# Attention and a gated feed-forward layer on one core: the mixture of v written in the queries' order by TensorE, w_spatial rounded on ScalarE, and new keys for the order of issue

## The chip, the cores and the metric

The kernel runs on one core of a Trainium2 chip. The metric is the device time of one execution in microseconds (us), as the median of several runs. A profile is one more execution, recorded by the hardware; its span runs from the first to the last recorded instruction. In the profile PE is TensorE, DVE is VectorE, ACT is ScalarE, POOL is GpSimd and SP is SyncE, which issues the DMAs.

## The reference

Eight batches of twelve heads attend over 448 positions with head size 64; the result, 448 x 768 for each batch, goes through a gated feed-forward layer. All inputs and outputs are float32.

```python
scores = matmul(q, k.T) / 8
scores = cap * tanh(scores / cap)
attn = exp(scores - max(scores)) / (sum + 1e-9)
x = matmul(attn, v)                      # heads side by side: (8, 448, 768)
h = maximum(x @ w_in, 0)                 # (8, 448, 1024)
u, v = h[..., :512], h[..., 512:]
v_n = (v - mean(v)) / sqrt(var(v) + 1e-6)
v_s = einsum('ts,bsd->btd', w_spatial, v_n) + b_spatial[None, :, None]
out = (u * v_s) @ w_out                  # (8, 448, 768)
```

## The kernel before

Two heads make a pair; there are 48 pairs, six to a batch. `pair_bnd` builds the work of a pair and `moe` that of a batch's feed-forward layer. Neither issues anything: each calls `add` with an engine, a duration, a key, what the task depends on and which buffers it takes. `Plan.order` then runs through a model of the engines and issues, on each engine, the ready task of least key, so that the keys, the durations and the buffer counts fix the order of instructions on every engine before the kernel runs. Keys come from the pair's number and a table (`BND_KEY`, with `KEY0` added in the first batch). TensorE works in two modes: attention matmuls on 64 x 64 tiles of the array (mode "K") and feed-forward matmuls on the whole array (mode "N"). The model adds `TURN` when the mode changes, and `STICK` to the key of a task that would change it.

The work of a pair, in blocks of 64 keys (seven blocks, `NC`), is this. The scores (line 548) go to the PSUM tile ps_s, of which there are two; ScalarE takes the tanh (line 555) and then, over half of the keys at a time, the exponential (line 560) into a tile tp. TensorE sums exp times v over the blocks into ps_x (line 570), of which there is one, and ScalarE copies it to xf (line 575). The order of the queries within qk2 is chosen on the host (`qp`, line 876), so that VectorE can find the maximum over keys by elementwise steps, a 32 x 32 transpose and a reduction (lines 590 to 600, tile red). The sum over keys is found in the same way, but in the first eight pairs (`PE_SUMS`) TensorE makes it with a matrix of ones (line 612, to ps_acc), and ScalarE copies it to sx (line 616, recorded at the helper's line 311). Maximum and sum cross the partitions by four small DMAs (md, dt, rd, rr), after which VectorE multiplies xf by rr (line 661), and xf is split into two rounded parts xg: a copy on ScalarE (line 662, recorded at line 311) and a difference on VectorE (line 663, recorded at line 307).

Since the queries come in another order than the output wants, the two copies out of PSUM put them back:

```python
out=xf.t.rearrange("p (i h b) -> p h b i", h=2, b=QB // 2), in_=x.t[:, :, :QH].rearrange("p h (b i) -> p h b i", i=32)
```

For the feed-forward layer of a batch TensorE makes u (lines 694 to 696), v (lines 716 to 721), the spatial product (lines 785 to 790) and the output (lines 810 to 812). Before the first of these the weights have to be split: w_in and w_out by `split_f64`, w_spatial by `split_f32`, whose four roundings to ws_h run on VectorE (line 338).

Of the kernel before, what the change touches and what calls it, by code (L numbers as in the profile page):

```python
# [42 lines left out]
class Plan:  # L43
# [7 lines left out]
    TURN, STICK = {"N": 200.0, "K": 150.0, "R": 190.0, "C": 145.0, "Q": 130.0}, 8.1  # L51
# [19 lines left out]
    def order(self):  # L71
# [35 lines left out]
        while done < len(self.tasks):  # L107
# [87 lines left out]
def gpc(n):  # L195
# [7 lines left out]
U_LEAD = 2  # L203
MOE_TAGS = {
    "xg": (XW, F32R, 8), "u": (448, F32, U_LEAD), "vh": (512, F32R, 4), "vl": (512, F32R, 4),
# [11 lines left out]
    "sx": (448, F32, 1), "v": (2 * NC * D, F32, 2), "tp": (2 * PW, F32, 4),  # L217
# [19 lines left out]
E_SEV = "A"  # L237


def attn_moe(ctx, tc, bounded, shared, qk, v, qk2, v2, cap, w_in, w_sp, w_out, out):  # L240
# [88 lines left out]
    def split_f32(key, c):  # L329
# [8 lines left out]
        b = add("V", dve2(S), key, lambda: nc.vector.tensor_copy(hi, t.t[:, :S]), [a], [t])  # L338
# [181 lines left out]
    def pair_bnd(b, hp, xf, rr):  # L520
# [3 lines left out]
        kk = lambda name, n=0: at + KEY[name] + KEY["step"] * n + (KEY0.get(name, 0.0) if b == 0 else 0.0)  # L524
# [7 lines left out]
        x, tps, exps, prev = Buf("x"), [], [], None  # L532

# [5 lines left out]
        for j in range(2):  # L539
            tp = Buf("tp")  # L540
# [62 lines left out]
        row = lambda y: y.rearrange("(e p c) -> p e c", e=2, c=QB)  # L603
# [289 lines left out]
```

## Time and profile before

| | us |
|---|---|
| median of 3 runs | 753.5 (752.08 to 755.51) |
| the profiled execution's own time | 750.37 |
| its span | 748.6 |
| TensorE busy in the span | 729.3 |
| VectorE busy | 616.5 |
| ScalarE busy | 495.7 |

The profiled execution lies 3.1 us under the median of the runs, and 1.8 us of its time lie around the span. A matmul in the profile begins before the one ahead of it has ended, so TensorE's busy time is not a sum of durations; the spacing from one start to the next is what a matmul costs in a row of them. Each attention matmul in the program is two matmul instructions in the profile, so a pair's 28 matmuls for scores, and its 28 for the mixture, are 56 there.

### The profile page before, as it was taken

How to read it: one execution, taken by the hardware profiler on the slowest of the kernel's cores; microseconds unless marked ns; L12 is line 12 of the kernel's file. 1: busy time of each engine (PE TensorE's matmuls, PEld its weight loads, DVE VectorE, ACT ScalarE, POOL GpSimd, SP SyncE). 2: the span in 40 equal slices, each digit the busy share in tenths (PEclk: the TensorE clock that was granted, in tenths of full speed). 3: DMA queues.
4: the chain of work that ended last, by engine and by line, in shares of the span. 5: the costliest groups of instructions: out<-in, count | busy, mean ns of one | idle time of the engine just before them, and what ended most of it. 6: DMA issues, size and time to landing. Idle time of an engine off the chain costs nothing.

```text
span 748.6 us, 18868 instructions
## 1 busy us (share of the span) xinstructions
PE 729.3 (97%) x7865; PEld 598.3 (80%) x7865; DVE 616.5 (82%) x1174; ACT 495.7 (66%) x658; POOL 62.4 (8%) x65
## 2 busy tenths in 40 slices
PE   7997999999999999999999999999999999999997
PEld 5865787886788878887788878888788877888896
DVE  4898899999999899867998599985999779986520
ACT  7999838669757584569855696557855698554321
POOL 3341211100100010000000001000010000100100
PEclk9999999999999999999999999999999999999999
DMA  7675613354222432234321352223322343112002
GB/s 247 183 219 170 230 47 126 95 166 138 76 66 86 144 103 76 65 113 138 114 63 36 135 160 77 66 87 128 115 65 72 125 133 115 42 28 89 13 2 79
DMA packets 51140, 79.22 MB, mean 106 GB/s; under 512 B 22882, under 2 KB 35684, under 8 KB 51044
## 3 DMA queue, kind: packets, MB, share of 16 engines
q1 hardware_dynamic: 51044, 77.91, 33.3%
q8 instruction: 64, 1.05, 0.6%
q14 instruction: 32, 0.26, 0.1%
HBM read 66.04 MB, written 11.81 MB: 104 GB/s over the span
## 4 chain that ended last, share of the span: by engine, by line
PE 67%; DVE 15%; DMA 11%; ACT 2%; issue 2%; POOL 1%; SPq 1%; DVEq 0%; ACTq 0%
PE ps_s L548 11%; PE ps_x L570 11%; DVE red L590 5%; PE ps_acc L810 4%; PE ps_acc L812 4%; PE ps_acc L811 4%; PE ps_acc L694 4%; PE ps_acc L695 4%; PE ps_acc L696 4%; PE ps_acc L719 3%; PE ps_acc L721 3%; PE ps_acc L720 3%; DMA rd<-dt 3%; DMA rr<-rd 3%; PE ps_acc L788 2%
## 5 line engine op out<-in xcount | busy, mean ns | idle before, releaser
L555 ACT ACTIVATE tp<-ps_s,capt 128x896 f32<-128x896 f32 x192 | 168.0, 911 | 20.6 <-PE ps_s L548 15.6
L548 PE MATMUL ps_s<-raw 64*64 64x224 f32 x2688 | 150.8, 355 | 8.3 <-ACT tp L555 8.1
L590 DVE TENSOR_TENSOR red<-red,tp 128x448 f32<-128x448 f32 (+1 forms) x176 | 148.0, 853 | 10.1 <-ACT tp L560 9.2
L560 ACT ACTIVATE tp<-tp,capt 128x1792 f32<-128x1792 f32 x96 | 154.2, 1606 | 2.2
L570 PE MATMUL ps_x<-tp,v 64*64 64x224 f32 x2688 | 145.5, 355 | 3.9 <-ACT xf L575 3.9
L548 PEld LDWEIGHTS ps_s<-raw 64*64 64x64 f32 x2688 | 98.1, 133 | 46.7 <-ACT tp L555 16.2
L570 PEld LDWEIGHTS ps_x<-tp,v 64*64 64x64 f32 x2688 | 103.6, 135 | 32.7 <-ACT xf L575 6.0
L590 DVE TENSOR_TENSOR red<-tp 128x896 f32<-128x896 f32 x88 | 93.1, 1076 | 22.6 <-ACT tp L560 22.6
L743 POOL TENSOR_TENSOR lst<-lst,capt 128x1 f32<-128x1 f32 x32 | 27.4, 857 | 561.3 <-DVE lst L741 547.1
L810 PE MATMUL ps_acc<-xg,wo_h 128*128 128x448 f32 x176 | 64.6, 367 | 0.1
L812 PE MATMUL ps_acc<-xg,wo_l 128*128 128x448 f32 x176 | 63.9, 363 | 0.0
L811 PE MATMUL ps_acc<-xg,wo_h 128*128 128x448 f32 x176 | 63.6, 361 | 0.0
L694 PE MATMUL ps_acc<-xg,wi_h 128*128 128x448 f32 x174 | 63.4, 364 | 0.0
L695 PE MATMUL ps_acc<-xg,wi_h 128*128 128x448 f32 x174 | 63.1, 363 | 0.0
L696 PE MATMUL ps_acc<-xg,wi_l 128*128 128x448 f32 x174 | 63.0, 362 | 0.0
L311 ACT COPY o<-ps_acc 128x448 f32<-128x448 f32 x44 | 23.4, 533 | 50.2 <-PE ps_acc L812 45.1
L598 DVE STREAM_TRANSPOSE red<-red 128x448 f32<-128x448 f32 x88 | 55.6, 634 | 0.8
L719 PE MATMUL ps_acc<-wi_h,xg 128*128 128x512 f32 x132 | 54.7, 414 | 0.0
L590 DVE TENSOR_TENSOR red<-red 128x448 f32<-128x448 f32 x88 | 53.7, 618 | 0.5
L575 ACT COPY xf<-ps_x 128x448 f32<-128x448 f32 x48 | 45.7, 951 | 12.0 <-DVE xg L307 5.1
L600 DVE TENSOR_REDUCE st<-red 128x14 f32<-128x448 f32 x88 | 51.5, 610 | 1.0
L720 PE MATMUL ps_acc<-wi_l,xg 128*128 128x512 f32 x132 | 52.2, 395 | 0.0
(116 smaller groups left out, 1147.7 us busy)
## 6 DMA issues: line engine op xcount, KB each, us to landing
raw<-in_qk SPq DMA_DIRECT2D x48, 448.0 KB, 3.9
v<-in_v SPq DMA_DIRECT2D x48, 448.0 KB, 4.1
rr<-rd SPq DMA_DIRECT2D x96, 112.0 KB, 2.8
out<-o SPq DMA_DIRECT2D x48, 224.0 KB, 2.0
w<-in_w_in SPq DMA_DIRECT2D x12, 512.0 KB, 4.7
xg<-in_w_out SPq DMA_DIRECT2D x12, 256.0 KB, 3.4
rd<-dt SPq DMA_DIRECT2D x48, 3.5 KB, 1.5
wy<-in_w_sp SPq DMA_DIRECT2D x3, 224.0 KB, 3.6
```

The source lines that it names most:

```text
L548: nc.tensor.matmul(ps.t[half_rows(h), e, c % 2 * QH:(c % 2 + 1) * QH], lhsT=raw.t[half_rows(e), S + c * D:S + (c + 1) * D], rhs=raw.t[half ...
L555: lambda o=g % 2 * PW, w=w, ps=ps, tp=tp: nc.scalar.activation(out=tp.t[:, o:o + 2 * w].rearrange("p (e q) -> p e q", e=2), in_=ps.t[:, :, ...
L560: lambda tp=tp, w=w: nc.scalar.activation(out=tp.t[:, :w], in_=tp.t[:, :w], func=AF.Exp, scale=ca), [ex], [tp],
L570: nc.tensor.matmul(x.t[half_rows(e), h, :QH], lhsT=vt.t[half_rows(h), (2 * c + e) * D:(2 * c + e + 1) * D], rhs=part(c, e)[half_rows(h)], ...
L590: tt = lambda o_, i0, i1, op=op: nc.vector.tensor_tensor(o_, i0, i1, op=op)
L694: nc.tensor.matmul(ps, lhsT=wi_h[:, c, fs], rhs=x[:, XH:], start=(c == 0), stop=False)
L695: nc.tensor.matmul(ps, lhsT=wi_h[:, c, fs], rhs=x[:, :S], start=False, stop=False)
L696: nc.tensor.matmul(ps, lhsT=wi_l[:, c, fs], rhs=x[:, XH:], start=False, stop=(c == NP - 1))
L719: nc.tensor.matmul(ps, lhsT=x[:, XH:][:, ts], rhs=wi_h[:, c, FH:], start=(c == 0), stop=False)
L810: nc.tensor.matmul(ps, lhsT=wo_h[:, c, ns], rhs=g[:, XH:], start=(c == 0), stop=False)
L811: nc.tensor.matmul(ps, lhsT=wo_h[:, c, ns], rhs=g[:, :S], start=False, stop=False)
L812: nc.tensor.matmul(ps, lhsT=wo_l[:, c, ns], rhs=g[:, XH:], start=False, stop=(c == 3))
```

## The change

Four things are changed. First, the matmuls of the mixture and of the sums write their output in the queries' own order: the host orders the queries so that each half of 224 stays together (`qp`), and the PSUM address steps by 7 elements, 28 bytes, from one column to the next (`inat`), where it stepped by one element before. The copies to xf and sx then read and write in order (sx in runs of seven elements), and the small DMA to rd moves runs of seven elements where it moved fourteen. Second, ScalarE rounds w_spatial. Third, the tile tp is split into tp for the first half of the keys and tq for the second, two buffers each in place of four, and u gets a third buffer. Fourth, the model of the engines and the keys have new numbers, and the second and the last batch have tables of their own beside the first.

```diff
-    TURN, STICK = {"N": 200.0, "K": 150.0, "R": 190.0, "C": 145.0, "Q": 130.0}, 8.1
+    TURN, STICK = {"N": 90.0, "K": 100.0, "R": 190.0, "C": 145.0, "Q": 130.0}, 12.24
...
-                    if e == "S":
+                    if e == "S" and took.dur:
                         dma = max(dma, took.end + 650.0) + took.lat + 300.0
-                        took.lat = dma + (1100.0 if took.lat > 1000.0 else 500.0) - took.end
+                        took.lat = dma + (1300.0 if took.lat > 1000.0 else 900.0) - took.end
...
-    "xg": (XW, F32R, 8), "u": (448, F32, U_LEAD), "vh": (512, F32R, 4), "vl": (512, F32R, 4),
+    "xg": (XW, F32R, 8), "u": (448, F32, 3), "vh": (512, F32R, 4), "vl": (512, F32R, 4),
...
-    "sx": (448, F32, 1), "v": (2 * NC * D, F32, 2), "tp": (2 * PW, F32, 4),
+    "sx": (448, F32, 1), "v": (2 * NC * D, F32, 2), "tp": (2 * PW, F32, 2), "tq": (PW + S, F32, 2),
...
+KEY1 = dict(ld=-4.24, vld=1.47, sc=-2.25, th=0.85, ex=-17.45, pv=-3.87, sm=-2.29, mx=-0.73, dn=-6.62, ev=-0.32, x=-5.3, moe=0.67, mv=-0.58)
+KEY7 = dict(ld=27.96, vld=8.74, sc=1.5, th=-0.21, ex=31.1, pv=18.57, sm=1.15, mx=0.16, dn=25.98, ev=42.09, x=22.77, moe=25.89, mv=8.24)
...
-        b = add("V", dve2(S), key, lambda: nc.vector.tensor_copy(hi, t.t[:, :S]), [a], [t])
+        b = add(E_WS, ct(E_WS, S), key, lambda: copy(E_WS, hi, t.t[:, :S]), [a], [t])
...
+        inat = lambda y: y.rearrange("p (i b) -> p b i", b=QB // 2)
+        hq = lambda y: y.rearrange("p (h q) -> p h q", h=2)
...
-                            nc.tensor.matmul(x.t[half_rows(e), h, :QH], lhsT=vt.t[half_rows(h), (2 * c + e) * D:(2 * c + e + 1) * D],
+                            nc.tensor.matmul(inat(x.t[half_rows(e), h, :QH]), lhsT=vt.t[half_rows(h), (2 * c + e) * D:(2 * c + e + 1) * D],
                                              rhs=part(c, e)[half_rows(h)], start=(c == 0), stop=(c == NC - 1))
...
-        z = add("A", act(S) + 420, kk("ev"), lambda: nc.scalar.copy(
-            out=xf.t.rearrange("p (i h b) -> p h b i", h=2, b=QB // 2), in_=x.t[:, :, :QH].rearrange("p h (b i) -> p h b i", i=32)), [prev],
-            [x, xf], [xf], name="xev")
+        z = add("A", act(S) + 45, kk("ev"), lambda: nc.scalar.copy(out=hq(xf.t), in_=x.t[:, :, :QH]), [prev], [x, xf], [xf], name="xev")
...
-                            nc.tensor.matmul(acc[h].t[half_rows(e), 0, :QH], lhsT=one[half_rows(h)], rhs=part(c, e)[half_rows(h)],
+                            nc.tensor.matmul(inat(acc[h].t[half_rows(e), 0, :QH]), lhsT=one[half_rows(h)], rhs=part(c, e)[half_rows(h)],
                                              start=(c == 0), stop=(c == NC - 1))
...
-            out=row(rd.t), in_=sec(0).rearrange("p (e c) -> p e c", c=QB)), [d], [dt], [rd], lat=XL)
+            out=row(rd.t), in_=sec(0).rearrange("p (e h b) -> p e h b", e=2, h=2)), [d], [dt], [rd], lat=XL)
...
-    qp = qt.reshape(B, H, D, 32, QB).transpose(0, 1, 2, 4, 3).reshape(B, H, D, S)
+    qp = qt.reshape(B, H, D, 2, 32, QB // 2).transpose(0, 1, 2, 3, 5, 4).reshape(B, H, D, S)
```

The numbers of matmuls, DMAs and vector instructions stay as they are, but for the four roundings that go from VectorE to ScalarE. The order changes everywhere. Three places follow; a count behind a row is of equal instructions in succession, 28 attention matmuls being one step of a pair.

On TensorE, in the middle of a later batch, the kernel before goes from the feed-forward matmuls (lines 785 to 790 and 694) to one pair's attention step and back. The rows are four attention rows between the last and the first feed-forward rows around them:

```order
L789 MATMUL ps_acc<-ws_l,vh 128x448
L790 MATMUL ps_acc<-ws_h,vl 128x448
L548 MATMUL ps_s<-raw_60 64x224 x16
L570 MATMUL ps_x<-tp,v 64x224 x16
L548 MATMUL ps_s<-raw_60 64x224 x12
L570 MATMUL ps_x<-tp,v 64x224 x12
L785 MATMUL ps_acc<-ws_l,vh 128x448
```

The changed kernel at the same point of a later batch (its lines are some five to seven further down: 555 for scores, 577 for the mixture, 791 to 796 for the spatial product):

```order
L796 MATMUL ps_acc<-ws_h,vl 128x448
L555 MATMUL ps_s<-raw_167 64x224 x12
L577 MATMUL ps_x<-tp,v 64x7x32 x16
L555 MATMUL ps_s<-raw_60 64x224 x16
L577 MATMUL ps_x<-tq,v 64x7x32 x12
L555 MATMUL ps_s<-raw_60 64x224 x12
L577 MATMUL ps_x<-tp,v 64x7x32 x16
L577 MATMUL ps_x<-tq,v 64x7x32 x12
L555 MATMUL ps_s<-raw_167 64x224 x16
L791 MATMUL ps_acc<-ws_l,vh 128x448
```

Where one visit held one pair's 56 matmuls, it now holds two pairs' 112, and the visits are fewer. Over the whole kernel TensorE goes from one mode to the other 83 times before and 61 times now.

On ScalarE, at the start, the kernel before has these rows after the two tanhs of the first half of pair 0 (tp is the scores' tile, sx the sums, xf the mixture):

```order
L560 ACTIVATE tp<-tp,capt 128x1792
L555 ACTIVATE tp<-ps_s,capt 128x896
L555 ACTIVATE tp<-ps_s,capt 128x448
L560 ACTIVATE tp<-tp,capt 128x1344
L555 ACTIVATE tp<-ps_s,capt 128x896 x2
L560 ACTIVATE tp<-tp,capt 128x1792
L311 COPY sx<-ps_acc 128x7x32 x2
```

And the changed kernel (562 is the tanh, 567 the exponential, 316 the copies):

```order
L567 ACTIVATE tp<-tp,capt 128x1792
L316 CAST ws_h<-wy 128x448
L562 ACTIVATE tq<-ps_s,capt 128x896
L316 CAST ws_h<-wy 128x448 x2
L562 ACTIVATE tq<-ps_s,capt 128x448
L562 ACTIVATE tp<-ps_s,capt 128x896
L567 ACTIVATE tq<-tq,capt 128x1344
```

Three of the four roundings of w_spatial now stand between the tanhs and exponentials of pair 0; the fourth comes after pair 2's.

On TensorE, in the last batch, the kernel before multiplies the sixth pair's part of x (xg_8290) into the first tile of v (ps_s_8258) after ten steps over the other five parts, which go to two tiles:

```order
L719 MATMUL ps_s_8279<-wi_h_156,xg_8213 128x512
L720 MATMUL ps_s_8279<-wi_l_157,xg_8213 128x512
L721 MATMUL ps_s_8279<-wi_h_156,xg_8213 128x512
L719 MATMUL ps_s_8258<-wi_h_156,xg_8290 128x512
L720 MATMUL ps_s_8258<-wi_l_157,xg_8290 128x512
L721 MATMUL ps_s_8258<-wi_h_156,xg_8290 128x512
```

The changed kernel does so (xg_8320 into ps_s_8245) only after all four tiles have had their five other parts:

```order
L721 MATMUL ps_acc_8314<-wi_h_159,xg_8274 128x512
L722 MATMUL ps_acc_8314<-wi_l_160,xg_8274 128x512
L724 MATMUL ps_s_8245<-wi_h_159,xg_8320 128x512
L725 MATMUL ps_s_8245<-wi_l_160,xg_8320 128x512
L726 MATMUL ps_s_8245<-wi_h_159,xg_8320 128x512
```

Ahead of these rows, since the last scores of the last pair, the kernel before has 72 output matmuls, 28 of the mixture and 30 of v; the changed one has 28 of the mixture, 48 of the output, 28 of the mixture and 55 of v.

## Rows read from the trace of the kernel before

**Rows 1.** Windows: stretch, its us, busy us by engine (instructions), granted clock, DMA share, GB/s.

```profile
4.90:90.14 85.24, 75.66 (x1448) 57.05 (x1448) 73.65 (x134) 79.04 (x103) 29.09 (x20) 0.94 0.71 222
60.00:80.00 20.00, 14.69 (x236) 10.18 (x232) 17.51 (x36) 17.31 (x25) 5.42 (x3) 0.83 0.61 197
90.14:743.00 652.86, 650.04 (x6412) 540.09 (x6408) 542.02 (x1035) 414.60 (x553) 33.12 (x41) 1.00 0.29 91
```

**Rows 2.** TensorE's waits to 90.14 us: who for whom, total us, times, longest.

```profile
PE ps_s L548 <- ACT tp L555: 6.1, 4, 3.3
PE ps_x L570 <- ACT xf L575: 3.4, 2, 2.0
```

**Rows 3.** TensorE's waits after 90.14 us.

```profile
PE ps_s L548 <- ACT tp L555: 1.9, 4, 1.1
PE ps_x L570 <- ACT xf L575: 0.4, 1, 0.4
```

**Rows 4.** Groups of ScalarE by shape: count, busy us, mean ns of one, idle before.

```profile
L555 ACT ACTIVATE tp<-ps_s,capt 128x896 f32<-128x896 f32 x144 | 141.2, 1003 | 20.5 <-PE ps_s L548 15.6 <-DVE red L590 3.5 <-PE ps_x L570 1.1
L560 ACT ACTIVATE tp<-tp,capt 128x1792 f32<-128x1792 f32 x48 | 86.0, 1792 | 1.1
L560 ACT ACTIVATE tp<-tp,capt 128x1344 f32<-128x1344 f32 x48 | 68.2, 1420 | 1.1
L575 ACT COPY xf<-ps_x 128x448 f32<-128x448 f32 x48 | 45.7, 951 | 12.0 <-DVE xg L307 5.1 <-DVE dt L634 3.7 <-PE ps_x L570 2.8
L311 ACT COPY o<-ps_acc 128x448 f32<-128x448 f32 x44 | 23.4, 533 | 50.2 <-PE ps_acc L812 45.1 <-ACT xg L311 2.6 <-DMA out<-o 2.5
```

**Rows 5.** Timeline of TensorE around two mode changes: start us, duration us, instruction.

```profile
343.53 0.39 PE L720 MATMUL ps_acc<-wi_l,xg 128*128 128x512 f32 x1
343.76 0.40 PE L721 MATMUL ps_acc<-wi_h,xg 128*128 128x512 f32 x1
344.09 1.74 PE L548 MATMUL ps_s<-raw 64*64 64x224 f32 x32
345.65 2.83 PE L570 MATMUL ps_x<-tp,v 64*64 64x224 f32 x56
348.30 1.31 PE L548 MATMUL ps_s<-raw 64*64 64x224 f32 x24
349.55 0.50 PE L719 MATMUL ps_acc<-wi_h,xg 128*128 128x512 f32 x1
```

**Rows 6.** Timeline of ScalarE at 42 us: start us, duration us, instruction.

```profile
40.47 1.79 ACT L560 ACTIVATE tp<-tp,capt 128x1792 f32<-128x1792 f32 x1
42.16 0.92 ACT L575 COPY xf<-ps_x 128x448 f32<-128x448 f32 x1
42.88 0.98 ACT L311 COPY sx<-ps_acc 128x224 f32<-128x224 f32 x2
43.66 0.63 ACT L311 CAST wi_h<-wy 128x512 fp32r<-128x512 f32 x1
...
45.95 0.57 ACT L311 CAST xg<-xf 128x448 fp32r<-128x448 f32 x1 [0.75 <-DVE xf L661]
46.42 0.63 ACT L555 ACTIVATE tp<-ps_s,capt 128x448 f32<-128x448 f32 x1
46.95 0.23 ACT L311 CAST xg<-xf 128x64 fp32r<-128x64 f32 x1
```

**Rows 7.** Timeline of TensorE where the last pair's scores end.

```profile
671.57 0.56 PE L548 MATMUL ps_s<-raw 64*64 64x224 f32 x8
...
672.37 0.37 PE L811 MATMUL ps_acc<-xg,wo_h 128*128 128x448 f32 x1
672.57 0.37 PE L812 MATMUL ps_acc<-xg,wo_l 128*128 128x448 f32 x1
```

**Rows 8.** Timeline where that pair's x is first used.

```profile
696.21 0.63 DVE L307 TENSOR_TENSOR xg<-xf,xg 128x448 fp32r<-128x448 f32 x1 [0.63 <-ACT xg L311]
...
697.05 0.39 PE L721 MATMUL ps_s<-wi_h,xg 128*128 128x512 f32 x1
```

More of the change, by code (lines that the diff above doesn't have):

```diff
@@ L224 @@
 ANY_W_KEYS = 2.0, 0.5, 8.0, 9.0, 1.0
-BND_KEY = dict(ld=-9.15, vld=0.69, sc=-2.3, th=36.27, ex=-132.38, pv=-0.12, sm=8.79, mx=10.7, dn=-1.77, ev=-20.83, x=-6.67, moe=11.19, span=6.93, step=0.15, mv=-18.73)
-KEY0 = dict(ld=-49.29, vld=2.7, sc=-103.24, th=-27.84, ex=31.5, pv=-29.52, sm=-1.19, mx=-50.91, dn=-18.09, ev=-50.06, x=-27.36, moe=-7.29, mv=5.22)
+BND_KEY = dict(ld=-71.91, vld=-26.44, sc=-4.99, th=45.96, ex=-129.9, pv=-0.09, sm=23.74, mx=23.02, dn=-17.91, ev=-77.3, x=-0.5, moe=11.36, span=8.83, step=1.3, mv=-12.86)
+KEY0 = dict(ld=-10.07, vld=2.24, sc=-114.04, th=-22.5, ex=63.83, pv=-24.18, sm=-41.18, mx=-48.52, dn=-59.88, ev=-2.76, x=-23.04, moe=-10.0, mv=5.36)
+KEY1 = dict(ld=-4.24, vld=1.47, sc=-2.25, th=0.85, ex=-17.45, pv=-3.87, sm=-2.29, mx=-0.73, dn=-6.62, ev=-0.32, x=-5.3, moe=0.67, mv=-0.58)
+KEY7 = dict(ld=27.96, vld=8.74, sc=1.5, th=-0.21, ex=31.1, pv=18.57, sm=1.15, mx=0.16, dn=25.98, ev=42.09, x=22.77, moe=25.89, mv=8.24)
 BND_V_FIRST = 1
 WARM, WARM_N = 9, 512
-BND_W_KEYS = -3.23, 2.34, -35.92, 5.87, -12.54
+BND_W_KEYS = -26.38, 3.1, -30.55, 8.66, -10.67
 PE_SUMS = 8
@@ L244, in attn_moe, with own @@
     PS = bass.MemoryType.PSUM
+    def own(b, name):
+        return {0: KEY0, 1: KEY1, B - 1: KEY7}.get(b, {}).get(name, 0.0) if bounded else 0.0
     def pool(name, bufs, space=None):
@@ L523, in pair_bnd @@
         at = b * H + 2 * hp
-        kk = lambda name, n=0: at + KEY[name] + KEY["step"] * n + (KEY0.get(name, 0.0) if b == 0 else 0.0)
+        kk = lambda name, n=0: at + KEY[name] + KEY["step"] * n + own(b, name)
         raw, vt = Buf("raw"), Buf("v")
@@ L539, in pair_bnd @@
         for j in range(2):
-            tp = Buf("tp")
+            tp = Buf("tq" if j else "tp")
             for g in (2 * j, 2 * j + 1):
@@ L602, in pair_bnd @@
                 [st] if a == 0 else [], name="red3"))
-        row = lambda y: y.rearrange("(e p c) -> p e c", e=2, c=QB)
+        row = lambda y: y.rearrange("(e h p b) -> p e h b", e=2, h=2, p=32)
         sums = None
@@ L611, in ones @@
                         for e in range(2):
-                            nc.tensor.matmul(acc[h].t[half_rows(e), 0, :QH], lhsT=one[half_rows(h)], rhs=part(c, e)[half_rows(h)],
+                            nc.tensor.matmul(inat(acc[h].t[half_rows(e), 0, :QH]), lhsT=one[half_rows(h)], rhs=part(c, e)[half_rows(h)],
                                              start=(c == 0), stop=(c == NC - 1))
             def sev(h):
-                copy(E_SEV, sx.t.rearrange("p (i h b) -> p h b i", h=2, b=QB // 2)[:, h],
-                     acc[h].t[:, 0, :QH].rearrange("p (b i) -> p b i", i=32))
+                copy(E_SEV, sx.t.rearrange("p (i h b) -> p h i b", h=2, b=QB // 2)[:, h],
+                     acc[h].t[:, 0, :QH].rearrange("p (i b) -> p i b", i=32))
             sums = add("T", NC * QQ, kk("pv", 1) + 0.01, ones, exps, [u, w, *acc], acc, name="ones", mode="K")
-            sums = [add(E_SEV, act(QH) + 210 if E_SEV == "A" else dve(QH), kk("ev"), lambda h=h: sev(h), [sums], [acc[h], sx], [sx] if h == 0 else [], name="sev")
+            sums = [add(E_SEV, act(QH) + 60 if E_SEV == "A" else dve(QH), kk("ev"), lambda h=h: sev(h), [sums], [acc[h], sx], [sx] if h == 0 else [], name="sev")
                     for h in range(2)]
@@ L659, in pair @@
         g = Buf("xg")
-        k += KEY["x"] + (KEY0["x"] if b == 0 else 0.0) if bounded else 1.3
+        k += KEY["x"] + own(b, "x") if bounded else 1.3
         m = add(E_X[0], st2(E_X[0], 448), k, lambda: eng[E_X[0]].tensor_tensor(xf.t, xf.t, rr.t, op=ALU.mult), deps, [xf, rr], name="xmul")
@@ L675, in moe @@
     def moe(b, xs):
-        k0 = (b + 1) * H + KEY["moe"] + (KEY0["moe"] if bounded and b == 0 else 0.0)
+        k0 = (b + 1) * H + KEY["moe"] + own(b, "moe")
         step = KEY["span"] / 18.0
@@ L682, in moe @@
         tags = iter(["s", "s", "acc", "acc"] * 5 if bounded and b == B - 1 else ["acc"] * 18)
-        kv = lambda k: k + KEY["mv"] + (KEY0["mv"] if bounded and b == 0 else 0.0)
+        kv = lambda k: k + KEY["mv"] + own(b, "mv")
         def u_part(js):
@@ L766, in v_part @@
                 vs.append((vh, vl, s4, s5 if last else None))
+        lead = U_LEAD0 if bounded and b < V_FIRST else U_LEAD
         if b >= V_FIRST:
             v_part()
-            u_part(range(U_LEAD))
+            u_part(range(lead))
         else:
-            u_part(range(U_LEAD))
+            u_part(range(lead))
             v_part()
         for j in range(4):
-            if j and j + U_LEAD <= 4:
-                u_part([j + U_LEAD - 1])
+            if j and j + lead <= 4:
+                u_part([j + lead - 1])
             k = next(ks)
```

4 lines of the change are left out of this document (2 added, 2 removed).

## Prediction

> **What bounds the kernel now.** I read the windows first, since the share of busy time hides two quite different stretches. From 90.14 us on, where the first feed-forward matmul starts, TensorE is busy 650.0 of 652.9 us at the full granted clock, and its waits there come to some 2.3 us, on ScalarE's tanh and on its copy to xf [rows 1, 3]. In that stretch only three things can change the time: how long a matmul takes, how often the mode changes, and a new wait.
>
> Up to 90.14 us it is otherwise. From 4.90 to 90.14 us ScalarE is busy 79.0 of 85.2 us, TensorE 75.7 and VectorE 73.7 [rows 1]. TensorE's waits there are 9.5 us, all on ScalarE: 6.1 us for a tanh that frees a scores tile, 3.4 us for the copy that frees the only ps_x [rows 2]. Its mean clock is 0.94, and 0.83 from 60 to 80 us, where part of the time it had the lower of its two levels, 1.2 GHz, after such waits [rows 1]. ScalarE sets the pace of this first stretch, TensorE that of the rest.
>
> Prices: four matmul instructions on 64 x 64 tiles run together, and 56 of them (14 such fours) take from 345.65 to 348.30, which is 0.189 us a four, 2.65 us for a pair's scores or mixture [rows 5]. Feed-forward matmuls are 0.20 us apart at 448 columns and 0.23 at 512 [rows 5, 7].
>
> **The change, part by part.** *Mode changes.* From the scores at 348.30 (six fours, 1.14 us) to the feed-forward matmul at 349.55 is 1.25 us, so 0.11 over; from the matmul at 343.76 to the scores at 344.09 is 0.33 in place of 0.23, so 0.10 over [rows 5]. A change costs 0.105 us, and 22 fewer save **2.3 us**. This is TensorE's own time in the stretch that it bounds.
>
> *Copies on ScalarE.* The copy to xf takes 951 ns on average, but what follows starts before its end: 42.16 to 42.88 is 0.72 us. A ScalarE operation on as many elements that reads and writes in order is a cast to xg, 0.47 us to the next start (45.95 to 46.42); the copy of an output tile takes 533 ns by its mean [rows 4, 6]. So each copy costs 0.25 us less by starts, 0.42 by durations. I take the starts. Two copies to sx cost 0.78 us (42.88 to 43.66) [rows 6]; half of 0.47 each, for half the columns, would be 0.47, and because their writes still step every seven elements I take 0.58, which saves 0.2 us a pair. Eight pairs lie in the first stretch: 8 x (0.25 + 0.2) = 3.6 us off ScalarE, against four roundings of 448 columns at 0.47 = 1.9 us put on it. Net **1.7 us** where ScalarE sets the pace. The lower end: if the three roundings between the tanhs of pair 0 hold up its scores while everything else is waiting for them, 1.4 us come back, and the net is 0.3. The upper end is 8 x (0.42 + 0.3) - 1.9 = 3.9 us. The four roundings leave VectorE, which does not set the pace; I count that as nothing, and it would be 1.9 us too if VectorE did.
>
> *After 90 us.* ScalarE is not the bound there (414.6 of 652.9 us busy), but the 2.3 us of waits are all on it, and each has one or two copies ahead of it that get shorter by 0.25. I take **1.3 us** of them back, between 0 and 2.3.
>
> *The strided write.* No row of this trace has TensorE write PSUM with a step, so I bound it by rates. An attention matmul writes 224 columns in the 0.189 us of a four, one element per partition and bank in 0.84 ns; a feed-forward matmul writes 448 in 0.20 us, one in 0.45 ns, or two adjacent elements in 0.90 [rows 5, 7]. If the cost is per pair of neighbouring elements, which the step makes into one each, the strided write needs one access in 0.84 ns where the densest row already makes one in 0.90. It fits, and I take **0**. The other end is a write at half the pace, 0.189 us more for each four. The mixture has 672 fours and the sums in eight pairs 112, so that end is 784 x 0.189 = 148 us. The Trainium skill ("PSUM — Partial Sum Buffer", Specifications (TRN2)) speaks against this change: it gives PSUM lines of 8 bytes and says that any non-contiguous access pattern slows matmuls significantly. By that sentence the kernel gets much slower; the rates of the rows leave room for the step, and no run here shows one yet. It is the first rival.
>
> *Visits of two pairs.* A pair's exponentials used to be ready a visit ahead; now the third block of scores of a visit waits for tanhs of the same visit. TensorE reaches it after 1.14 + 1.51 + 1.51 + 1.14 + 1.14 + 2.65 = 9.1 us. ScalarE begins some 1.0 us into the visit and has until then a tanh and a half (0.90 + 0.53), an exponential (1.32), two tanhs (1.80), a copy (0.47), an exponential (1.69) and a tanh (0.90): 7.6 us, so it is done at 8.6, and 8.8 with the handoff (durations less the 0.1 us by which the next start overlaps) [rows 4, 6]. It fits with 0.3 us left, and would not with the copy as it was. I take **0**; the bound is the second rival.
>
> *The last batch.* From the end of the last scores (671.57 + 0.38) to that pair's x is 24.9 us, as VectorE ends it at 696.84, and its first use is at 697.05: the kernel just gets by [rows 7, 8]. Now 28 + 28 attention matmuls, 48 of output and 55 of v stand in between: 5.3 + 9.7 + 12.8 + 0.3 = 28.1 us. So 3.2 us are to spare, which also covers the DMA to rd, whose pieces are half as long. Nothing is gained by it, because nothing waited. What is late next is the last tile of v, now finished with the first one; u follows on TensorE for 36 x 0.20 = 7.2 us, and I count this as even.
>
> *No cost elsewhere.* The split into tp and tq keeps four buffers, and the third buffer of u gives room only.
>
> Sum: 2.3 + 1.7 + 1.3 = 5.3 us off the profiled execution's 750.4 (span 748.6 and 1.8 around it) gives 745.1. The median of the runs lies 3.1 us above that execution, so **748.2 us**. A change of 0.5%, 3.8 us, is about what a measurement of this kernel can tell from none.
>
> **The rivals.** *The strided write is slow* (slower; place: the mixture and the sums). At half the pace: 748 + 148 = 896 us. It decides early: with 5.3 us of gain, 7 ns on each of the 784 fours (4%) bring the time back to that of before, and 12 ns (6%) make it slower by 0.5%. Against it speak the rates; for it, that no row of this trace holds a strided write, so nothing measured excludes it. The sentence of the Trainium skill ("PSUM — Partial Sum Buffer", Specifications (TRN2)) is on its side. Chance 0.13.
>
> *Visits of two pairs wait.* Eleven visits hold 112 attention matmuls. If a cast to xg and its small one (0.47 + 0.13) come between, the 0.3 us are gone and 0.3 us are lost; with VectorE late to free tp it may be 0.5: 11 x 0.5 = 5.5 us, about 753.7 us. It takes the place of the waits removed. Chance 0.13.
>
> *Only the mode changes count.* The roundings on ScalarE at the start, and a new order there with its own waits, eat the copies' gain: 751.2 us. For it speaks that TensorE waits for ScalarE from the first tanh on. Chance 0.17.
>
> *The first stretch is repaired.* ScalarE is idle 6.2 us of it, and TensorE loses up to 0.06 x 85.2 = 5.1 us to the lower clock [rows 1]. With an order that keeps both busy another 5 us go: 743 us. For it speaks that the mixture now comes before the sums, so that ps_x is freed earlier. Chance 0.20.
>
> **How the numbers follow.** The forecast has the rest, 0.37; its own range, from the bounds of the copies and of the waits, is 744 to 751. The range of 741 to 755.5 takes in the last three rivals but for their ends, and leaves out the slow write (0.13) and some 0.06 at the ends. Faster than 749.7: 0.29 of the forecast, 0.20 of the first stretch, 0.04 of the mode changes alone, 0.04 of the waiting visits (they may wait less), 0.57 together, and I say 0.58. Slower than 757.3: the slow write 0.13 and 0.03 of waiting visits, 0.16. The rest is 0.26.
>
> **What would show it.** The fours of the mixture and of the sums still 0.189 us apart, or not: that alone can make the prediction badly wrong. The copy to xf near 0.53 us on average. TensorE's waits up to the first feed-forward matmul under 9.5 us, and that matmul before 90 us by about two. In the middle, waits of TensorE for a tanh inside the visits would show the second rival, and none would show the working right; 0.105 us at each of 61 mode changes. In the last batch no wait before the last pair's x. The forecast would be wrong, too, if the lower clock came at other places: each microsecond at 1.2 GHz that TensorE has work in costs half of one.

## The result and the profile after

| | us |
|---|---|
| before, median of 5 runs | 753.5 (752.08 to 755.51) |
| after, median of 5 runs | 746.8 (743.99 to 749.32) |
| ratio after to before | 0.9912, 95% interval 0.9888 to 0.9936 |
| the profiled execution of after, its own time | 743.99 |
| its span | 742.0 |

The changed kernel is 0.9% faster: 746.8 us, 1.4 under the 748.2 forecast and inside its range, a gain of 6.7 us where 5.3 were forecast. The whole interval lies beyond the 0.5% that a measurement can tell. The profiled execution lies again below the median of the runs, by 2.8 us.

The same three windows, with the first feed-forward matmul now at 83.66 us (it was at 90.14), answer to [rows 1].

```profile
4.90:83.55 78.65, 70.63 (x1401) 52.75 (x1400) 63.44 (x119) 73.24 (x100) 17.14 (x18) 0.98 0.72 218
60.00:80.00 20.00, 17.23 (x356) 12.93 (x350) 17.05 (x34) 18.46 (x27) 3.84 (x3) 1.00 0.70 204
83.55:737.00 653.45, 649.26 (x6460) 543.91 (x6456) 543.91 (x1046) 406.01 (x562) 32.90 (x44) 1.00 0.31 94
```

The first stretch is 6.6 us shorter. It also holds less: 12 fours of attention (48 records, of which the window misses one: 1448 became 1401) now lie behind its end, 2.3 us of TensorE's work at 0.189 a four. The granted clock from 60 to 80 us is 1.00, where it was 0.83. The long stretch is no shorter.

TensorE's waits in the first stretch, and then those behind it, answer to [rows 2, 3].

```profile
PE ps_s L555 <- ACT tq L562: 7.0, 5, 2.6
PE ps_s L555 <- ACT tp L562: 0.4, 1, 0.4
...
PE ps_acc L699 <- ACT xg L316: 1.3, 1, 1.3
PE ps_acc L699 <- DVE stg L736: 1.0, 1, 1.0
PE ps_acc L796 <- DVE vl L312: 0.7, 1, 0.7
PE ps_acc L816 <- DVE o L801: 0.4, 1, 0.4
```

The wait for ps_x is gone, and no wait inside a visit of two pairs is in the list. The waits behind the first stretch are new ones. The sixteenth feed-forward matmul, the first that needs the last pair's xg, waits for it; later ones wait for stg, vl and o. Behind that xg stand a transfer, VectorE's product and ScalarE's cast, one after the other:

```profile
86.86 0.63 DVE L666 TENSOR_TENSOR xf<-xf,rr 128x448 f32<-128x448 f32 x1 [1.26 <-DMA rr<-rd]
...
87.58 0.71 ACT L316 CAST xg<-xf 128x448 fp32r<-128x448 f32 x2 [3.72 <-DVE xf L666]
...
88.20 0.47 PE L699 MATMUL ps_acc<-xg,wi_h 128*128 128x448 f32 x1 [1.26 <-ACT xg L316]
```

The groups of ScalarE by shape answer to [rows 4].

```profile
L562 ACT ACTIVATE tp<-ps_s,capt 128x896 f32<-128x896 f32 x96 | 91.9, 999 | 12.9 <-PE ps_s L555 6.8 <-PE ps_x L577 5.3 <-DVE red L595 0.6
...
L582 ACT COPY xf<-ps_x 128x448 f32<-128x448 f32 x48 | 25.5, 531 | 7.8 <-DVE xg L312 5.0 <-PE ps_x L577 2.5
L316 ACT COPY o<-ps_acc 128x448 f32<-128x448 f32 x44 | 23.3, 532 | 42.4 <-PE ps_acc L818 40.8 <-issue 1.1 <-ACT xg L316 0.5
...
L316 ACT COPY sx<-ps_acc 128x224 f32<-128x224 f32 x16 | 5.0, 368 | 0.8 <-PE ps_acc L617 0.7
```

The copy to xf takes 531 ns in place of 951, as the copy of an output tile does; the copy to sx takes 368 in place of the 574 of before:

```profile
L311 ACT COPY sx<-ps_acc 128x224 f32<-128x224 f32 x16 | 7.6, 574 | 0.6 <-PE ps_acc L612 0.6
```

The timeline of TensorE in a visit of two pairs shows the strided write.

```profile
343.73 1.69 PE L577 MATMUL ps_x<-tp,v 64*64 64x224 f32 x32
345.24 1.69 PE L555 MATMUL ps_s<-raw 64*64 64x224 f32 x32
346.75 0.56 PE L577 MATMUL ps_x<-tq,v 64*64 64x224 f32 x8
```

Eight fours of the mixture, written with the step, take 1.51 us, as do eight fours of scores, written without it: 0.189 us a four in both.

Where the 6.6 us of span went I read by adding up the distances from each start of a TensorE matmul to the next, from the first attention matmul to the last matmul of the program. The usual step of its kind is taken off each, and what is over is put down to a recorded wait, to a change of mode, or, in attention matmuls of over 450 ns, to the lower clock.

| us | before | after |
|---|---|---|
| usual steps | 703.8 | 704.1 |
| waits up to the first feed-forward matmul | 9.6 | 8.0 |
| waits behind it | 2.8 | 4.0 |
| lower clock | 7.1 | 3.1 |
| mode changes (83, then 61) | 8.5 | 6.4 |
| the rest | 5.9 | 5.6 |
| sum | 737.7 | 731.2 |

By this table mode changes gave 2.1 us, waits 0.4, and the lower clock 4.0, which the prediction did not have as a term. Each column is one execution. The experiments ask whether these are causes.

### The profile page after: what moved, and what is told of

Same layout as the page of the kernel before. It is cut to its first block, busy times and chain, and to the rows that moved or that the text cites. A ratio compares the mean times of both kernels' runs of the same rounds, so it can differ in the third digit from the quotient of the medians.

```text
span 742.0 us, 18882 instructions
## 1 busy us (share of the span) xinstructions
PE 723.6 (98%) x7865; PEld 597.9 (81%) x7865; DVE 608.1 (82%) x1170; ACT 481.2 (65%) x662; POOL 50.2 (7%) x65
## 4 chain that ended last, share of the span: by engine, by line
PE 82%; DVE 8%; DMA 6%; ACT 2%; issue 1%; SPq 1%; POOL 0%; DVEq 0%; ACTq 0%; POOLq 0%
PE ps_s L555 15%; PE ps_x L577 15%; PE ps_acc L816 5%; PE ps_acc L817 5%; PE ps_acc L818 5%; PE ps_acc L699 4%; PE ps_acc L724 4%; PE ps_acc L701 4%; PE ps_acc L700 4%; PE ps_acc L725 3%; PE ps_acc L726 3%; DMA rr<-rd 3%; DVE red L595 3%; PE ps_acc L794 2%; PE ps_acc L796 2%; PE ps_acc L795 2%
## 5 line engine op out<-in xcount | busy, mean ns | idle before, releaser
L595 DVE TENSOR_TENSOR red<-red,tq 128x896 f32<-128x896 f32 (+1 forms) x176 | 146.2, 846 | 43.1 <-ACT tq L567 42.9
L562 ACT ACTIVATE tp<-ps_s,capt 128x896 f32<-128x896 f32 x96 | 91.9, 999 | 12.9 <-PE ps_s L555 6.8
L567 ACT ACTIVATE tp<-tp,capt 128x1792 f32<-128x1792 f32 x48 | 86.5, 1802 | 0.6
L577 PE MATMUL ps_x<-tp,v 64*64 64x224 f32 x1536 | 81.8, 349 | 0.0
L562 ACT ACTIVATE tq<-ps_s,capt 128x896 f32<-128x896 f32 x96 | 74.7, 822 | 10.0 <-PE ps_s L555 9.2
L577 PEld LDWEIGHTS ps_x<-tp,v 64*64 64x64 f32 x1536 | 58.4, 133 | 14.9 <-issue 0.6
L567 ACT ACTIVATE tq<-tq,capt 128x1344 f32<-128x1344 f32 x48 | 68.1, 1419 | 1.3
L577 PE MATMUL ps_x<-tq,v 64*64 64x224 f32 x1152 | 63.5, 349 | 0.0
L748 POOL TENSOR_TENSOR lst<-lst,capt 128x1 f32<-128x1 f32 x32 | 24.4, 765 | 567.4 <-DVE lst L746 489.2
L316 ACT CAST xg<-xf 128x448 fp32r<-128x448 f32 (+1 forms) x96 | 35.0, 404 | 28.6 <-DVE xf L666 23.1
```

What stands on the lines that cost most here:

```text
L562: lambda o=g % 2 * PW, w=w, ps=ps, tp=tp: nc.scalar.activation(out=tp.t[:, o:o + 2 * w].rearrange("p (e q) -> p e q", e=2), in_=ps.t[:, :, ...
L567: lambda tp=tp, w=w: nc.scalar.activation(out=tp.t[:, :w], in_=tp.t[:, :w], func=AF.Exp, scale=ca), [ex], [tp],
L577: nc.tensor.matmul(inat(x.t[half_rows(e), h, :QH]), lhsT=vt.t[half_rows(h), (2 * c + e) * D:(2 * c + e + 1) * D], rhs=part(c, e)[half_rows ...
L595: tt = lambda o_, i0, i1, op=op: nc.vector.tensor_tensor(o_, i0, i1, op=op)
```

## The experiments

Medians are compared with runs of the kernel before on the same chip, given beside each. "First matmul" is the start of the first feed-forward matmul in the profile.

**The layout alone.** The new layout in the order of before, and with w_spatial still rounded on VectorE.

```diff
-                            nc.tensor.matmul(x.t[half_rows(e), h, :QH], lhsT=vt.t[half_rows(h), (2 * c + e) * D:(2 * c + e + 1) * D],
+                            nc.tensor.matmul(inat(x.t[half_rows(e), h, :QH]), lhsT=vt.t[half_rows(h), (2 * c + e) * D:(2 * c + e + 1) * D],
...
-            out=xf.t.rearrange("p (i h b) -> p h b i", h=2, b=QB // 2), in_=x.t[:, :, :QH].rearrange("p h (b i) -> p h b i", i=32)), [prev],
+            out=hq(xf.t), in_=x.t[:, :, :QH]), [prev],
...
```

> The layout alone (strided write by TensorE, copies in order, halves of the queries, small DMA) in the order of issue of the kernel before, word for word. Theory: the fours of mixture and sums stay 0.189 us apart, the copy to xf falls from 951 to about 530 ns, and ScalarE, which paces the first stretch, has about 3.6 us less there with no roundings added; the first feed-forward matmul comes 1.5 to 3.5 us before 90.1 and the time is 750 to 752 us (0.995 to 0.998 of before). Rival, that the whole gain is the order's: 753.5 us, ratio 1.000. Rival, that most of it is the layout's: under 749 us.

Measured: 754.45 against 754.17, ratio 1.0008 (0.9991 to 1.0024). The copies are short (523 and 362 ns), and nothing is gained. First matmul at 91.38 us, against 90.14. ScalarE's waits up to there show where the saving went.

```profile
ACT tp L557 <- PE ps_s L550: 5.1, 4, 4.4
ACT xg L311 <- DVE xf L663: 4.1, 3, 1.8
ACT tp L557 <- PE ps_x L572: 1.8, 1, 1.8
```

In before the wait for VectorE's xf was 1.1 us in all:

```profile
ACT xg L311 <- DVE xf L661: 1.1, 2, 0.7
```

ScalarE does 6.0 us less of copies up to that point (9.1 in place of 15.1), and its idle time grew by 4.9: from 6.2 by [rows 1] to 11.1, 75.4 busy of 86.5.

**The order alone.** The order of after, w_spatial on ScalarE, the layout of before.

```diff
-                            nc.tensor.matmul(inat(x.t[half_rows(e), h, :QH]), lhsT=vt.t[half_rows(h), (2 * c + e) * D:(2 * c + e + 1) * D],
+                            nc.tensor.matmul(x.t[half_rows(e), h, :QH], lhsT=vt.t[half_rows(h), (2 * c + e) * D:(2 * c + e + 1) * D],
...
-    qp = qt.reshape(B, H, D, 2, 32, QB // 2).transpose(0, 1, 2, 3, 5, 4).reshape(B, H, D, S)
+    qp = qt.reshape(B, H, D, 32, QB).transpose(0, 1, 2, 4, 3).reshape(B, H, D, S)
```

> The changed kernel's order of issue, with the layout of before (contiguous write by TensorE, copies out of PSUM that reorder). Theory: 61 mode changes as in the changed kernel, 2.1 us less than before; ScalarE has 3.6 us more in the first stretch than the changed kernel, and in the visits of two pairs TensorE waits 0.1 to 0.5 us for a tanh in several of the eleven, since the copy of 0.72 us does not fit; 749 to 752 us. Rival, that the order makes all of it: 746 to 747.5 us and no waits inside visits.

Measured: 749.98 against 754.17, ratio 0.9949 (0.9929 to 0.9969); first matmul at 86.88 us. So the layout alone is worth 0, the order alone 4 us, both 7: the short copies are worth about 3 us in the new order and nothing in the old. (What is called the order here holds the roundings on ScalarE, the split of tp and the third buffer of u as well; only the roundings are taken by themselves, below.)

In the profiles the first matmul lies 3.2 us behind after's. Of these, 1.7 are a slower stretch behind the wait for a tanh at 45 us: 64 attention matmul instructions take 4.77 us there, and 3.08 in after, with a granted clock from 40 to 60 us of 0.91 against 1.00. First after, then the order alone:

```profile
45.43 1.74 PE L555 MATMUL ps_s<-raw 64*64 64x224 f32 x32 [1.66 <-ACT tq L562]
...
45.66 2.90 PE L555 MATMUL ps_s<-raw 64*64 64x224 f32 x32 [2.22 <-ACT tq L562]
```

VectorE's waits up to 82 us differ between the two orders. First the kernel before, in which it waits for transfers and for GpSimd alone:

```profile
DVE ws_h L338 <- DMA wy<-in_w_sp: 5.5, 3, 4.6
DVE dt L634 <- DMA dt<-md: 3.2, 3, 1.8
DVE wy L380 <- POOL wy L376: 1.1, 2, 0.6
DVE xf L661 <- DMA rr<-rd: 0.9, 1, 0.9
```

Then the order alone, in which it waits for exponentials of ScalarE:

```profile
DVE red L595 <- ACT tp L567: 6.2, 1, 6.2
DVE red L595 <- ACT tq L567: 4.3, 2, 4.1
DVE dt L639 <- DMA dt<-md: 1.9, 3, 0.8
```

After has 6.0 and 4.0 in the two upper rows. In the order of before VectorE has no wait for ScalarE in this list, and with the short copies ScalarE waits 4.1 us for it. The 10 us of the new order are not the opposite of that: the two long waits end at 10.2 and 15.4 us, so they are for the first pair's exponentials, where before had the 5.5 us for w_spatial's transfer. Behind them VectorE waits at most 1.0 us at a time for ScalarE, and these lists do not show which engine sets the pace from there on.

**The roundings of w_spatial back on VectorE,** in after, at the same place of the order. It was run twice, the second time beside the changed kernel on one chip.

```diff
-    b = add(E_WS, ct(E_WS, S), key, lambda: copy(E_WS, hi, t.t[:, :S]), [a], [t])
+    b = add(E_WS, ct(E_WS, S), key, lambda: copy("V", hi, t.t[:, :S]), [a], [t])
```

> The changed kernel with the four roundings of w_spatial issued on VectorE at the same place of the order. Theory: TensorE's wait of 2.6 us at 8.6 us, which two of the roundings on ScalarE lengthen, falls to about 1.6; ScalarE has 1.9 us less to do in the first stretch; 745 to 746 us, 1 to 1.9 us under the changed kernel. Rival, that VectorE's queue is late in turn (maxima of pair 0, weights of w_in): the same time or up to 1 us more, the first feed-forward matmul not before 83.5 us.

> The changed kernel with the four roundings of w_spatial on VectorE at the same place of its order, for a profile nearer to its median than the one that the first such run left, and a comparison with the changed kernel on the same chip. Theory: the roundings cost ScalarE 1.9 us where it sets the pace and VectorE has room (5.8 of 15.1 us busy up to 20 us), so 1.5 to 3.5 us under the changed kernel (about 743.5), with the first feed-forward matmul 1 to 2 us earlier than the changed kernel's. Rival: the 3.5 us of the first comparison were a luckier clock; then the two are within 1 us.

Measured: first 743.33 against 754.17, ratio 0.9855 (0.9837 to 0.9872), then 745.26 against 752.96, ratio 0.9898 (0.9876 to 0.992). The profile of the first is of its slowest execution, and has the first matmul at 85.47 us, 1.5 to 1.8 behind the 83.66 and 83.97 of the changed kernel's two profiles. In that of the second it is at 81.83 us, 1.8 to 2.1 before them, and the window up to there shows ScalarE shorter by 2.3 and VectorE fuller by 2.7 than in after:

```profile
4.90:81.83 76.93, 69.88 (x1400) 53.97 (x1400) 66.12 (x124) 70.97 (x96) 16.79 (x18) 0.98 0.74 225
```

But on the one chip that both ran on, the time is the same (745.03 and 745.26). The 3.5 us of the first comparison did not come again. Two us in the first stretch are what one profile of two shows, so neither that the roundings cost them there nor that moving them shortens the whole is shown. In that one profile TensorE is still 1.7 us ahead of after's at 300 us, at the same matmul, and 0.5 behind at 492. That is no more than what two executions of one kernel differ by: the two profiles of the changed kernel itself drift 2.3 us apart behind the first matmul.

**The changed kernel again,** on that chip.

> The changed kernel itself on this chip, for a second profile and as the measure for the other runs of this call. Median 745 to 748. If the theory is right that its runs spread with how often TensorE falls to 1.2 GHz after a wait, the span is lower where the granted clock is higher, and the second profile shows such a stretch at other places than 12 us; the steps of mixture and sums stay at 0.189 us a four in every stretch at full clock.

Measured: 745.03 against 752.96, ratio 0.9886 (0.9862 to 0.991). First matmul at 83.97 us. The sums of the table above are here 8.6 and 4.9 us for waits up to and behind it, 3.7 for the lower clock, 6.4 for mode changes. So the new waits behind the first stretch, 4.0 and 4.9, belong to the kernel and not to one execution. (Of the 4.9, two are for a tanh, 0.7 and 0.3 us, both in visits shorter than two pairs.) That the span falls with the granted clock did not hold: its five spans of 741.8 to 744.5 had 0.997, 0.994, 0.993, 0.995 and 0.997, in this order.

**Long copies in the first batch only, and in the others only.** The order of after; `old(b)` picks the layout of before. The edit is that of the first run; in the other the condition is `n > 0`.

```diff
+old = lambda n: n == 0
...
-    inat = lambda y: y.rearrange("p (i b) -> p b i", b=QB // 2)
+    inat = lambda y: y.rearrange("p (i b) -> p b i", b=QB // 2) if not old(b) else y
...
```

> The changed kernel, order and all, but the six pairs of the first batch have the layout of before, so that their copies on ScalarE are long again (about 0.95 and 0.58 us); 42 pairs keep the short copies. Theory: the order alone was 3.2 us slower than order and layout together because the first stretch, up to the first feed-forward matmul, goes at ScalarE's pace. Six long copies to xf (0.25 us each by starts) and twelve to sx (0.1 each) are 2.7 us there, so the median should lie 2 to 3 us over the changed kernel (by 746.8: 749 to 750), and the first feed-forward matmul should come 2 to 3 us later than 83.7 us. Rival: the long copies hurt in the visits of two pairs, which are all later; then this run is within 1 us of the changed kernel on the same chip.

> The mirror image: the first batch has the short copies, the other 42 pairs the layout of before with the long ones. Theory (the first stretch goes at ScalarE's pace): 747 to 748, at most the 1.3 us that waits after the first stretch can give, and the first feed-forward matmul near 83.7 us. Rival (the visits of two pairs do not fit with long copies): 11 visits by 0.3 us and more, 3.3 us, about 750, with waits of TensorE for a tanh inside the visits.

Measured, against 745.03 of the changed kernel: 746.55 with the long copies first (to before 0.9923, 0.9894 to 0.9952), 747.95 with the long ones later (0.9939, 0.9912 to 0.9965). First matmul at 85.13 and 84.97 us, 1.0 to 1.5 us behind the changed kernel's two. The later copies that could count for this are those of the two pairs of the second batch that lie ahead of the first matmul. But the delay does not last. At the sixteenth feed-forward matmul, which waits for the last pair's xg in the changed kernel, the two are at 88.24 and 88.33 us, and the changed kernel's profiles at 88.20 and 88.25; the order alone, with all copies long, is at 90.73. And with the long copies first 1.7 us of delay are again a slower stretch behind the wait at 45.6 us (granted clock 0.91 from 40 to 60 us). The rival asked for waits inside the visits, and the waits of TensorE behind the first matmul, with the long copies later, have none of over 0.3 us for a tanh:

```profile
PE ps_acc L803 <- DVE vl L313: 0.6, 1, 0.6
PE ps_acc L707 <- DVE xg L313: 0.4, 1, 0.4
PE ps_s L556 <- ACT tp L563: 0.3, 1, 0.3
```

By this profile the visits fit with the long copies too. The place that the theory gave is not shown either: by the profiles neither half costs anything at 88 us. Of the medians, the 1.5 us with the long copies first are within the overlap of the two intervals, and the 2.9 us with the long ones later are just clear of it (0.9912 to 0.9965, against 0.9862 to 0.991). Where the short copies gain their 3 us stays open.

**The casts to xg of the first batch on VectorE,** so that ScalarE no longer stands at them; with the layout alone, and with nothing else changed in before.

```diff
+        E_C, E_C2 = ("V", "V") if bounded and b == 0 else (E_X[1], E_X[3])
...
-        c = add(E_X[1], ct(E_X[1], 448), k, lambda: copy(E_X[1], g.t[:, XH:], xf.t), [m], [xf], [g], name="xh")
+        c = add(E_X[1], ct(E_X[1], 448), k, lambda: copy(E_C, g.t[:, XH:], xf.t), [m], [xf], [g], name="xh")
...
```

> The layout alone in the order of before, and the two casts to xg of each pair of the first batch on VectorE at the same place of the order, where they follow the product that they read. The layout alone took 6 us of copies off ScalarE in the first stretch, and the time stayed. Theory: ScalarE takes its work in order, and stood at these casts for that product (4.1 us in all against 1.1 before), which itself waited for the transfer to rr; tanhs queued behind it. With the casts off its queue the gain appears: the wait is gone, ScalarE is idle 3 to 5 us less up to the first feed-forward matmul, that matmul comes 2 to 4 us before 91.4 us, and the median falls 2 to 3 us under before. Rival: the pace lies with VectorE or the transfers themselves; then the wait moves to other instructions, and the time is that of before or, with 3 us more on VectorE, longer.

> The kernel before with the same casts of the first batch on VectorE, as the measure for the run above. Theory (ScalarE's work in order sets the pace, with long copies there is little to win): its wait of 1.1 us for the product and the 4.5 us of casts leave ScalarE, so 1 to 3 us may go too; the run with the short copies is 2 us or more under this one. Rival: this run and the one above are equal within 1 us, so the copies are worth nothing in this order even then.

Measured: 755.3 and 754.18 against 752.13, ratios 1.0033 (1.0011 to 1.0055) and 1.0029 (1.0009 to 1.0048); first matmul at 92.69 and 91.84 us. The theory fell and the rival held. With the short copies ScalarE now waits for VectorE at other instructions:

```profile
ACT tp L557 <- PE ps_s L550: 4.8, 4, 4.1
ACT xf L577 <- DVE xg L307: 3.4, 1, 3.4
ACT wi_h L311 <- DVE wy L383: 2.1, 3, 1.2
```

Work taken off ScalarE and put on VectorE made the kernel slower in this order, and the short copies were still worth nothing. VectorE and what it waits for set the pace of the first stretch in before.

**TensorE's waits filled,** in before at three of them and in after at two, by matmuls into columns that nobody reads; in after `FILL` is `{0: 6, 4: 4}`, by pairs.

```diff
+FILL = {0: 5, 6: 5, 7: 8}
...
+    for _ in range(FILL.get(b * NP + hp, 0) if blocks[-1] == NC - 1 else 0):
+        nc.tensor.matmul(ps.t[:, 0, QH:2 * QH], lhsT=raw.t[:, S:S + 128], rhs=raw.t[:, :QH], start=True, stop=True)
```

> The kernel before, with 18 extra matmuls (128x224, float32, into columns of a scores tile that nobody reads) where TensorE stood still: five behind the scores of the first pair, five behind those of the seventh (the wait that ended at 62.3 us), eight behind those of the eighth (the wait that ended at 75.4 us). They lengthen no wait if they take 0.37 us each. Theory: the half-pace stretches behind the last two waits (62.3 to 65.4 and 75.9 to 79.1 us in the profile of before) come of TensorE standing still before them; with the waits filled, both are gone, the loss at half pace up to the first feed-forward matmul falls from 6.0 to 3 us or less, and the time falls by 1 to 3 us (750 to 752.5 on this chip), since ScalarE may take part of it back. Rival: the lower level has another cause (the load on the engine, say); then the stretches stay where they are, and the time is the same or up to 2 us longer.

> The changed kernel with ten such extra matmuls in its two longest waits: six behind the scores of the first pair (the wait that ended at 11.5 us), four behind those of the fifth (45.4 us). Theory: the half-pace stretch from 12.0 to 14.9 us is gone, and the time is 0 to 1.5 us under the changed kernel's 745 to 747, since ScalarE sets the pace there. Rival: the stretch stays, and the time is the changed kernel's or up to 1 us more.

Measured: before filled 752.57 against 752.22, ratio 1.0006 (0.9984 to 1.0028). Its timeline of TensorE, with the extra matmuls in line 553:

```profile
59.77 2.16 PE L553 MATMUL ps_s<-raw 128*128 128x224 f32 x10
61.88 2.88 PE L573 MATMUL ps_x<-tp,v 64*64 64x224 f32 x56
...
69.98 3.29 PE L553 MATMUL ps_s<-raw 128*128 128x224 f32 x16
76.51 0.99 PE L549 MATMUL ps_s<-raw 64*64 64x224 f32 x16 [3.24 <-ACT tp L558]
```

In the profile of before the same mixture came behind a standstill, and took 4.54 us:

```profile
62.31 4.54 PE L570 MATMUL ps_x<-tp,v 64*64 64x224 f32 x56 [2.03 <-ACT xf L575]
```

The window up to the first matmul (at 91.22 us) now has the full clock, where [rows 1] had 0.94:

```profile
4.90:91.22 86.32, 79.68 (x1486) 64.00 (x1485) 71.69 (x133) 78.27 (x102) 29.17 (x20) 1.00 0.71 221
```

The standstill before the mixture is filled, and the lower clock behind it is gone. The last of the three was only moved: TensorE stands still for 3.24 us before 76.51, about as long as in before:

```profile
75.43 1.29 PE L548 MATMUL ps_s<-raw 64*64 64x224 f32 x16 [3.28 <-ACT tp L555]
```

Behind it the granted clock is another, though. From 75 to 80 us, first before, then before filled:

```profile
75.00:80.00 5.00, 4.57 (x60) 3.31 (x64) 4.45 (x8) 3.84 (x6) 2.59 (x2) 0.66 0.68 253
...
75.00:80.00 5.00, 3.49 (x72) 2.71 (x76) 4.43 (x8) 4.97 (x8) 3.13 (x2) 1.00 0.69 243
```

So the standstill alone does not bring the lower clock, and these runs do not show what else it takes.

Taking the lower clock away gains nothing in before: the time is the same (more than 1.2 us of gain lies outside the interval), and the first matmul is no earlier. ScalarE's wait for VectorE's xf up to 91 us is longer, 3.6 us where it was 1.1:

```profile
ACT xg L312 <- DVE xf L664: 3.6, 3, 2.3
```

After filled: 745.33 against 752.22, ratio 0.9906 (0.9878 to 0.9933), so the changed kernel's time; the half-pace stretch at 12 us is gone, and another stands at 77.9 us, behind a wait of 2.0. Its first matmul is at 87.02 us, 3.4 us behind after's. The same feed-forward matmul that after has at 120.33 us is 0.6 us behind, and the one at 205.32 is 0.5 us ahead: the delay at the first matmul is made up behind it.

**What a step costs where matmuls are denser.** After, with 72 bf16 matmuls of 448 columns at its start; the fp32 tile `ps` is written in order, with a step of 2, in order, with a step of 7, in order.

```diff
+    by = lambda b: ps[:, :448].rearrange("p (i b) -> p b i", b=b)
...
+    nc.tensor.matmul(by(2), lhsT=warm[:, :128], rhs=warm[:, :448], start=True, stop=True)
...
```

> The changed kernel with 72 extra bf16 matmuls of 128 x 448 before it starts: 24 that write PSUM in order, 12 with a step of 2 elements, 12 in order, 12 with a step of 7, 12 in order. Nothing else is changed; the time is longer by these. It measures the disputed write at one element in about 0.42 ns, twice the pace of the attention matmuls. If the cost is one access for each pair of neighbours: in order about 0.19 us apart at the full clock, stepped about 0.37. If a step costs nothing at any pace: 0.19 for all. If a step slows matmuls even at half the pace, the stepped ones are beyond 0.37.

Measured, in the timeline of TensorE (granted clock 1.00 in this window; lines 862 and 866 have the steps 2 and 7):

```profile
9.89 4.67 PE L862 MATMUL wps<-warm 128*128 128x448 bf16 x12
14.36 2.48 PE L864 MATMUL wps<-warm 128*128 128x448 bf16 x12
16.67 4.67 PE L866 MATMUL wps<-warm 128*128 128x448 bf16 x12
21.14 2.48 PE L868 MATMUL wps<-warm 128*128 128x448 bf16 x12
```

From 14.36 to 16.67 is 2.31 us for 12 in order, 0.193 us each or 0.43 ns an element. From 9.89 to 14.36 and from 16.67 to 21.14 is 4.47 us, 0.373 us each or 0.83 ns an element, for step 2 as for step 7. (The time of this one run, 764.75, holds the added matmuls.)

## Why the prediction was right, point by point

*Strided write, 0 us.* Right, and the runs fit the reason given, a cost for each pair of neighbouring elements: a step of 2 costs what a step of 7 costs, 0.83 ns an element, about twice the 0.43 in order. The attention matmul brings one element in 0.84 ns, so it has just enough room. The sentence of the Trainium skill ("PSUM — Partial Sum Buffer", Specifications (TRN2)) that any non-contiguous pattern slows matmuls significantly holds for the bf16 matmuls here, by a factor of 1.9, and does not hold for the attention matmuls, whose 0.189 us a four did not change; the measurement decides.

*Mode changes, 2.3 us.* Right by the sums: 61 of them, 2.1 us less, 0.105 us each, in both profiles of the changed kernel; no run changes their number alone. This is the one term that lies in the stretch that TensorE bounds.

*Copies on ScalarE, net 1.7 us.* The step that failed is "ScalarE sets the pace of this first stretch", with the four roundings on VectorE counted as nothing because it "does not set the pace". I read it from the busy time (79.0 against 73.7 us) and from TensorE's waits, which are all on ScalarE. But VectorE stood still for nothing but transfers and GpSimd, and ScalarE, given less to do, waited for VectorE: 4.1 us where it had been 1.1. In that order the copies' 3.6 us are worth 0, as the layout alone and the two runs with the casts moved show. In the new order they are worth about 3 us by the medians. By which path is argued and not shown. VectorE has 63.4 us of work ahead of the first feed-forward matmul in place of 73.7, which would leave the pace to ScalarE. But of the 3.2 us by which the first matmul comes earlier with the short copies (86.88 to 83.66), 1.7 are lower clock, and neither half of the copies alone shows a cost at 88 us. The roundings' 1.9 us are not shown either: one profile has 1.8 to 2.1, the other the opposite, and the medians are equal on one chip. The rival of the repaired first stretch was half right: the order shortened it, though ScalarE is hardly less idle (5.4 us, from 78.65 less 73.24, against 6.2).

*Waits after 90 us, 1.3 us back.* Wrong in sign: the old ones did go, but 2.8 us became 4.0 and 4.9 in the two profiles. The last pairs of the first batch now end later against the feed-forward work, which starts earlier, and its sixteenth matmul finds xg not ready.

*Visits of two pairs, 0 us,* and *the last batch, 0 us.* Right: no wait in either, in both profiles. The spare time of 0.3 us was reckoned too small, since no wait showed with the long copies either.

*The lower clock* was no term, and the sums show 4.0 us less of it. In before it is no cause: with its half-pace stretches gone the time was the same, and ScalarE waited longer for VectorE. In the new order that is not settled: two profiles have 1.7 us of lower clock behind 45 us, the first matmul comes later in both, and in one of them the delay is gone at 88 us. For the same reason the 1.6 us of waits up to the first feed-forward matmul are no separate gain: both follow from how early ScalarE and VectorE are done.

The account that stands: 2.1 us from the mode changes by the sums, and the rest from the new order and from the short copies, which gain only in that order. That the order does so by taking the pace of the first stretch from VectorE fits the runs in the order of before, and is not shown for the new one. By the sums of the first two profiles the first stretch gave 4.6 us (6.9, less the 2.3 of moved work) where the forecast had 1.7, and behind it 1.2 us of waits came on where the forecast took 1.3 off. Two misses nearly cancelled, so that the total was so near is in part luck. What stays open is how much of a gain ahead of the first matmul is kept: after filled came there 3.4 us late, and its span of 743.1 us lies between those of the changed kernel's two profiles, 742.0 and 744.5.

## What to carry to other kernels

Ask of each engine not only how busy it is but whom it would wait for if it had less to do: here 6 us taken off the busier engine turned into waits for a less busy one and were worth nothing until the order had been changed. Two edits that are worth 0 and 4 us apart can be worth 7 together, so price an edit in the order in which it will run. The start of a later stage in one profile is not a gain yet: 1.3 to 3.4 us of delay there were made up behind it, three times. A matmul that takes a PSUM element no faster than a step allows, 0.84 against 0.83 ns here, can write in the consumer's order for nothing; read the time per element from the profile first.

## What the runs showed of the hardware

A step of 2 fp32 elements in a matmul's PSUM write costs as much as a step of 7: 0.373 us for 448 bf16 columns in place of 0.193, at the full clock. For the attention matmuls on 64 x 64 tiles the step of 7 costs nothing. A ScalarE copy of 448 fp32 columns whose SBUF write steps by 14 elements at each one takes 951 ns, and 531 in order; one of 224 columns fell from 574 to 368 ns when its write stepped only between runs of seven. Extra matmuls at three standstills of TensorE kept the granted clock at 1.00 up to 91 us, where it had been 0.94, with 0.83 from 60 to 80; behind a standstill of 3.24 us that was left, the granted clock from 75 to 80 us was 1.00, and behind one of 3.28 us in the kernel before it was 0.66.
